# Local-global attention feeding a routed FFN: the first batch without zero-padded queries

## The chip, the cores and the metric

One core of a Trainium2 chip. The metric is the device time of one launch in microseconds, median of the runs shown. A profiled execution also has a span, from the first to the last instruction of the program; times inside it are counted from the span's start.

## The reference, cut to what matters

```python
# q_l, k_l, v_l: [8, 8, 512, 64]; q_g, k_g, v_g: [8, 8, 32, 64]; window 32
s_ll = where(|i - j| <= 32, scale * q_l @ k_l.T, -1e9)      # local rows: a band of keys
s_l  = concat([scale * q_l @ k_g.T, s_ll])                  # and the 32 global keys
out_l = softmax(s_l) @ concat([v_g, v_l])
out_g = softmax(scale * q_g @ concat([k_g, k_l]).T) @ concat([v_g, v_l])
x = concat([out_g, out_l]) per batch, heads side by side    # [4352, 512]
# greedy routing of the 4352 tokens to 8 experts of equal capacity 544, by x @ w_gate,
# then per expert out = relu(x_e @ w1) @ w2
```

## The kernel before, in words

The program has three parts in time: attention (to about 213 us of the span), routing (to about 244 us), and the eight expert FFNs. Each part needs the whole of the one before it.

Attention goes by pairs of heads, (batch b, pair q), q from 0 to 3, so 32 pairs. The host lays out queries and keys of a pair transposed in one array (`qk`: 64 partitions for each head), and the values with the windows of keys side by side (`ve`). For each pair GpSimd spreads the keys into a tile `kx` (three copies, line 117) and makes a shifted copy of the values, `vo` (lines 131 and 132).

The local queries of a head are 16 blocks of 32, and each block meets 128 keys (its own, both neighbours' and the global ones). The scores S of a pair are made in one of two ways:

- `Pair.scores`: for each block and each head one matmul of 64 partitions (the head's 64 dimensions) with 32 query columns: 32 matmuls in tiles of 64x32, which write the two S tiles (one for each head) in turns.
- `Padded.scores`: the queries lie in a tile `qz` of 128 partitions, head 0's in the upper half and head 1's in the lower one, with zeros beside them, so that one matmul of 128 partitions with 64 columns makes a block for both heads: 16 matmuls. GpSimd fills `qz` with two more copies for each such pair (line 121). There are two `qz` tiles, zeroed once at the start.

Which pair is which is said by `pads(b, q)`. A float32 matmul shows in the trace as two MATMUL and two LDWEIGHTS rows, a transpose as one of each.

After the scores VectorE subtracts, masks and takes the row maxima (line 197), ScalarE does the exponentials (line 202), TensorE transposes them (line 92), ScalarE and VectorE copy the transposed halves out of PSUM (line 353, 355), TensorE multiplies with the values (`outs`, from `ve` and `vo`), and VectorE divides by the row sums. Global queries of two pairs go together (`Glob`, tiles `pg`, `pgt`), and `Gate` turns finished rows and multiplies them with the gate weights.

The pairs are staged by hand in the loop over `st`: in stage st TensorE makes the scores of pair st+1, transposes pair st, and multiplies pair st-1 with its values, in that order. Each engine runs its instructions in the order in which they are written.

Loads and stores are issued by SyncE. `pe()` counts TensorE's instructions, 4 for a matmul and 2 for a transpose; when the count passes 194 and then every further 256, the instruction there is noted, and the next loads that `hand()` issues wait until it has run. So the loads go at a pace that the TensorE program sets. Buffers: six each of `qk` and `ve`, four each of `kx` and `vo`, four PSUM tiles S and four OT.

Of the kernel before, what the change touches and what calls it, by code (L numbers as in the profile page):

```python
# [68 lines left out]
def attention(ctx, tc, A, consts, xd, ident, L, nbatch, rt=None):  # L69
# [29 lines left out]
    def load_qk(b, p):  # L99
        t = ld.tile([128, 2 * QW], F32, name="qk", bufs=6)  # L100
        w = kx[(b * NP + p) % NK]
        move(t, A["qk"][b, p])
        k, qk[b, p] = t[:, QW:], (t, w)
        z = padded[b, p] = qz[(b * NP + p) // 2 % NZ] if pads(b, p) else None
        pd = list(w.ap[0])
        own = (ap_of(w[:, 128:192], 0, [pd, [160, 8], [1, 64]]), k[:, :SL].rearrange("p (a b) -> p a b", b=64))
        nxt = (ap_of(w[:, 224:256], 0, [pd, [160, 7], [1, 32]]),
               k[:, 64:SL].rearrange("p (a b) -> p a b", b=64)[:, :, 0:32])
        glo = (ap_of(w[:, 32:64], 0, [pd, [160, 8], [224, 2], [1, 32]]),
               k[:, None, None, SL:].to_broadcast([128, 8, 2, 32]))  # L110

        def spread(*engines):
            for e, (o, i) in zip(engines, (own, nxt, glo)):
                if e is nc.scalar:
                    e.activation(o, i, AF.Copy)
                else:
                    e.tensor_copy(o, i)  # L117
            if z is not None:
                for h in range(2):
                    r = slice(64 * h, 64 * h + 64)  # L120
                    nc.gpsimd.tensor_copy(z[r, :, h, :], t[r, :SL].rearrange("p (j i) -> p j i", i=32))
        return spread
# [10 lines left out]
        return spread  # L133

    def pads(b, q):
        return q % 2 == 0 and b + q > 0

    padded = {}
    qz = [ac.tile([128, NW, 2, 32], F32, name=f"qz{i}") for i in range(NZ)]
# [303 lines left out]

    ns = len(P)
    pairs = [(Padded if pads(*x) else Pair)(*x) for x in P]
    globs, need = {}, list(range(ns))
    for b in range(nbatch):
# [928 lines left out]
```

## Time and profile before

| | |
|---|---|
| runs, us | 689.93, 690.57, 693.05; median 690.57 |
| profiled execution | 688.41 us, span 686.6 us |
| mean granted TensorE clock | 0.974 of full speed |
| TensorE busy | 93% of the span |
| TensorE share of the chain that ended last | 76%; VectorE 13%, DMA 4%, issue 3%, ScalarE 2% |

The profiled execution lies 2.2 us below the median. "Issue" is time in which an engine waited for nothing that the profile shows.

### The profile page before, as it was taken

To read this page: it belongs to the slowest core of one execution; us is meant where nothing else is said; L and a number is where in the kernel's file an instruction comes from. 1 tells how busy PE (TensorE), PEld (TensorE's weight loads), DVE (VectorE), ACT (ScalarE), POOL (GpSimd) and SP (SyncE) were. 2 spreads that over 40 slices of the span, in tenths; PEclk is the share of its full clock that TensorE was granted. 3 is DMA by queue.
4 is the path that set the end of the run, shared out by engine and by line. 5 is a ranking of instruction groups with operands and counts; after the bars stand their busy time and mean duration, and the time that the engine had idled before them with its cause. 6 is when DMAs were issued, how large, how long until landed. Compare 5 with 4: busy or idle time off the path is not lost.

```text
span 686.6 us, 21729 instructions
## 1 busy us (share of the span) xinstructions
PE 635.3 (93%) x8854; PEld 543.9 (79%) x8854; DVE 488.2 (71%) x1988; ACT 315.1 (46%) x863; POOL 248.3 (36%) x321
## 2 busy tenths in 40 slices
PE   7889998899894289999999999999999999999996
PEld 7778876777773179879879978978977988988985
DVE  4697876776787788889988887978977961741510
ACT  5677877767760034344433433443432451642411
POOL 7877687673530050241141142142232143221011
PEclk9999999999998589999999999999999999999999
DMA  8585876776412170243334324325324325522001
GB/s 311 196 286 200 259 242 228 236 234 228 145 59 91 43 262 7 73 155 150 129 98 151 125 85 169 128 81 169 127 81 154 139 71 204 168 89 86 16 20 47
DMA packets 27253, 98.54 MB, mean 144 GB/s; under 512 B 5648, under 2 KB 5904, under 8 KB 23056
## 3 DMA queue, kind: packets, MB, share of 16 engines
q0 software_dynamic: 10640, 52.44, 22.3%
q1 hardware_dynamic: 16512, 44.70, 19.1%
q8 instruction: 70, 1.15, 0.7%
q14 instruction: 31, 0.25, 0.1%
HBM read 79.30 MB, written 17.83 MB: 141 GB/s over the span
## 4 chain that ended last, share of the span: by engine, by line
PE 76%; DVE 13%; DMA 4%; issue 3%; ACT 2%; POOL 0%; SPq 0%; POOLq 0%; DVEq 0%; ACTq 0%
PE H L1228 26%; PE Y L1254 25%; PE S L89 7%; PE OT L92 6%; PE OT L89 6%; PE R L716 3%; PE H L1054 2%; DVE p L197 2%; PE Y L1244 2%; DMA xg<-xd,idx 1%; DVE xs L232 1%; DMA qk<-in_qk_dram 1%; DMA w1r<-in_w_dram,widx 1%; DMA w2r<-in_w_dram,widx 1%; DVE pt L355 1%
## 5 line engine op out<-in xcount | busy, mean ns | idle before, releaser
L1228 PE MATMUL H<-xh,w1h 128*128 128x272 f32 (+2 forms) x512 | 149.2, 292 | 0.9 <-ACT xh L1027 0.8
L1228 PE MATMUL H<-xh,w1l 128*128 128x272 f32 (+2 forms) x512 | 149.7, 293 | 0.3 <-DVE w1l L641 0.3
L1228 PE MATMUL H<-xl,w1h 128*128 128x272 f32 (+2 forms) x512 | 148.6, 291 | 0.2 <-DVE xl L641 0.2
L1254 PE MATMUL Y<-w2h,hh 128*128 128x512 f32 x256 | 104.1, 407 | 0.0
L1254 PE MATMUL Y<-w2h,hl 128*128 128x512 f32 x256 | 103.3, 403 | 0.0
L1254 PE MATMUL Y<-w2l,hh 128*128 128x512 f32 x256 | 103.2, 403 | 0.0
L1231 ACT ACTIVATE hh<-H 128x272 fp32r<-128x272 f32 (+2 forms) x128 | 50.9, 398 | 113.2 <-PE H L1228 108.5
L1228 PEld LDWEIGHTS H<-xh,w1h 128*128 128x128 f32 x512 | 96.7, 189 | 1.7 <-ACT xh L1027 1.1
L1228 PEld LDWEIGHTS H<-xl,w1h 128*128 128x128 f32 x512 | 96.4, 189 | 0.8 <-DVE xl L641 0.6
L1228 PEld LDWEIGHTS H<-xh,w1l 128*128 128x128 f32 x512 | 96.6, 189 | 0.4 <-DVE w1l L641 0.4
L202 ACT ACTIVATE p<-p,nm 128x128 f32<-128x128 f32 x256 | 78.1, 398 | 2.5 <-DVE nm L197 2.5
L1014 POOL DMA_INDIRECT xg<-xd,idx x40 | 39.6, 989 | 103.2 <-DVE idx L641 47.9
L197 DVE CUSTOM_DVE_ANT_0 p<-S,mask 128x128 f32<-128x128 f32 x256 | 58.1, 286 | 20.2 <-PE S L89 17.7
L641 DVE SCALAR_TENSOR_TENSOR hl<-H,hh 128x272 fp32r<-128x272 f32 (+2 forms) x128 | 54.9, 434 | 20.5 <-ACT h L1233 14.0
L641 DVE TENSOR_TENSOR w2l<-w2r,w2h 128x512 fp32r<-128x512 f32 x64 | 41.8, 684 | 30.6 <-ACT w2h L1027 30.2
L1190 ACT ACTIVATE y<-Y 128x512 f32<-128x512 f32 x32 | 19.2, 599 | 94.8 <-PE Y L1254 80.9
L117 POOL COPY kx<-qk 128x512 f32<-128x512 f32 (+1 forms) x93 | 46.0, 530 | 43.8 <-DMA qk<-in_qk_dram 26.3
L1066 POOL DMA_INDIRECT out_dram<-y,idx x32 | 32.3, 1010 | 76.7 <-ACT y L1190 40.0
L1254 PEld LDWEIGHTS Y<-w2h,hh 128*128 128x128 f32 x256 | 48.3, 189 | 10.3 <-issue 1.6
L1254 PEld LDWEIGHTS Y<-w2h,hl 128*128 128x128 f32 x256 | 48.3, 189 | 9.2
L1254 PEld LDWEIGHTS Y<-w2l,hh 128*128 128x128 f32 x256 | 48.4, 189 | 8.9
L1027 ACT ACTIVATE w1h<-w1r 128x512 fp32r<-128x512 f32 x64 | 37.1, 624 | 35.3 <-DMA w1r<-in_w_dram,widx 35.3
(183 smaller groups left out, 1311.0 us busy)
## 6 DMA issues: line engine op xcount, KB each, us to landing
qk<-in_qk_dram SPq DMA_DIRECT2D x32, 544.0 KB
ve<-in_vw_dram SPq DMA_DIRECT2D x32, 520.0 KB
xd<-xs SPq DMA_DIRECT2D x32, 256.0 KB
xg<-xd,idx POOLq DMA_INDIRECT x40, 3.4
mask<-in_mask_dram SPq DMA_DIRECT2D x1, 512.0 KB
cf<-in_cf_dram POOLq DMA_DIRECT2D x1, 512.0 KB, 7.4
xd<-xg SPq DMA_DIRECT2D x16, 32.0 KB
gx<-xd POOLq DMA_DIRECT2D x8, 64.0 KB, 3.6
```

Source lines behind the costliest of these rows:

```text
L89: return pe(nc.tensor.matmul(*args, **kw), 4)
L92: return pe(nc.tensor.transpose(*args), 2)
L117: e.tensor_copy(o, i)
L197: nc.vector.tensor_tensor_reduce(s.p[h][:, c, :], s.st[h][:, c, :], mask[:, s.band(h, c), :], -SCALE, BIG, ALU.add, ALU.min, s.nm[h][:, c: ...
L202: nc.scalar.activation(s.p[h][:, c, :], s.p[h][:, c, :], AF.Exp, bias=s.nm[h][:, c:c + 1], scale=-1.0)
L641: return op(*args, **kw)
L1014: nc.gpsimd.indirect_dma_start(out=dst, out_offset=None, in_=src, element_offset=off, in_offset=bass.IndirectOffsetOnAxis(ap=idx, axis=0))
L1027: nc.scalar.activation(hi, raw, AF.Copy)
L1066: nc.gpsimd.indirect_dma_start(out=out, out_offset=bass.IndirectOffsetOnAxis(ap=rt.rows(ph, t)[:n], axis=0), in_=y[:n], in_offset=None)
L1228: nc.tensor.matmul(p, w[d][:, fs], x[:, d, q], start=(k == 0), stop=(k == 11))
L1231: nc.scalar.activation(hh[:, f, q], p, AF.Relu)
L1254: nc.tensor.matmul(p, h[:, f, q], w[f], start=(f + k == 0), stop=(f + k == 9))
```

## The change

`pads(b, q)` was true for every even pair but the very first, (0, 0). It is now true for even pairs from the second batch on. So it alters one pair, (0, 2), the third of the program, which becomes a `Pair` where it was a `Padded`. With it go its two copies into `qz`, its mask slices are those of the first third of `mask`, and its two halves are heads where they were halves of the sequence. `qz` tiles and their zeroing stay.

```diff
     def pads(b, q):
-        return q % 2 == 0 and b + q > 0
+        return q % 2 == 0 and b > 0
```

On TensorE, at the third group of scores, the tiles named are keys (`kx`), queries (`qk`, or padded `qz`), exponentials (`p`, `pg`):

```order
 L89 MATMUL S<-kx_103,qk 32x32 x2
 L92 MATMUL OT<-ident,p 128x128 x8
-L89 MATMUL S<-kx_104,qz_97 64x128 x16
+L89 MATMUL S<-kx_104,qk 32x128 x32
 L92 MATMUL OT<-ident,p 128x128 x4
 L92 MATMUL OT<-ident,pg_106 128x128 x6
```

Sixteen matmuls become 32, at the same place; in the trace 32 MATMUL rows become 64, and everything behind them stands 32 such rows, or 64 instructions, later in TensorE's stream.

On GpSimd, at the copies for pair (0, 2) and the shifted values of pair (0, 0):

```order
 L117 COPY kx_104<-qk 128x7x32
 L117 COPY kx_104<-qk 128x8x2x32
-L121 COPY qz_97<-qk 64x16x32 x2
 L131 COPY vo_98<-ve 128x1040
 L132 COPY vo_98<-ve 32x2x455
```

Two copies go, nothing else moves on this engine in attention.

On SyncE, the first place at which the order of loads differs (after the first store of global rows, `xd<-xg`):

```order
 L95 DMA ve<-in_vw_dram 128x1040 x2
 L349 DMA xd<-xg 4x32x64
+L95 DMA qk<-in_qk_dram 128x1088
+L95 DMA ve<-in_vw_dram 128x1040
 L95 DMA qk<-in_qk_dram 128x1088 x2
-L95 DMA ve<-in_vw_dram 128x1040 x2
 L349 DMA xd<-xg 4x32x64
```

Since `pe()` counts 64 more from pair (0, 2) on, the marks fall on instructions that stand earlier, and `hand()` takes the loads in another order from there on.

## Rows read from the trace of the kernel before

**Rows 1.** The page: TensorE's busy time and instructions.

```profile
PE 635.3 (93%) x8854; PEld 543.9 (79%) x8854; DVE 488.2 (71%) x1988; ACT 315.1 (46%) x863; POOL 248.3 (36%) x321
```

**Rows 2.** Busy time by stretch (us:us length, engines, PEclk, DMA share, GB/s).

```profile
33.00:213.40 180.40, 164.70 (x4675) 135.48 (x4653) 139.66 (x779) 129.34 (x404) 109.64 (x164) 1.00 0.63 208
213.40:244.20 30.80, 10.36 (x219) 7.70 (x219) 23.89 (x95) 2.12 (x4) 3.10 (x4) 0.56 0.16 53
```

**Rows 3.** TensorE in order of time (start, length, engine, line, [idle before]).

```profile
5.49 1.16 PE L89 MATMUL S<-kx,qk 64*32 64x128 f32 x64
12.25 3.54 PE L89 MATMUL S<-kx,qz 128*64 128x128 f32 x32 [1.99 <-POOL qz L121]
18.45 2.08 PE L89 MATMUL S<-kx,qk 64*32 64x128 f32 x80
22.85 0.41 PE L89 MATMUL OT<-ve,pgt 128*32 128x64 f32 x16
25.58 0.22 PE L89 MATMUL OT<-vo,pt 128*32 128x65 f32 x1 [1.91 <-issue]
26.04 3.47 PE L89 MATMUL S<-kx,qz 128*64 128x128 f32 x32
37.89 1.97 PE L89 MATMUL S<-kx,qz 128*64 128x128 f32 x32
...
112.34 0.22 PE L89 MATMUL OT<-vo,pt 128*32 128x65 f32 x1 [2.00 <-issue]
```

**Rows 4.** GpSimd in order of time, the first 22 us.

```profile
9.49 1.49 POOL L117 COPY kx<-qk 128x512 f32<-128x512 f32 x3 [2.41 <-DMA qk<-in_qk_dram]
10.92 1.28 POOL L121 COPY qz<-qk 64x512 f32<-64x512 f32 x2
...
14.50 1.48 POOL L117 COPY kx<-qk 128x512 f32<-128x512 f32 x3 [0.19 <-DMA qk<-in_qk_dram]
...
17.93 0.71 POOL L654 DMA_DIRECT2D cf<-in_cf_dram  x1
...
20.11 1.28 POOL L121 COPY qz<-qk 64x512 f32<-64x512 f32 x2
```

**Rows 5.** Granted clock (the number after POOL) and DMA share by stretch.

```profile
12.25:15.50 3.25, 3.25 (x30) 3.25 (x32) 0.93 (x8) 1.72 (x6) 2.99 (x5) 0.50 0.93 384
...
25.80:29.10 3.30, 3.30 (x43) 3.13 (x35) 1.69 (x11) 0.04 (x1) 3.18 (x6) 0.50 0.63 200
```

**Rows 6.** The whole program's instruction queue (packets, MB, share).

```profile
q8 instruction: 70, 1.15, 0.7%
```

**Rows 7.** Busy time from one code stall to the fourth after it.

```profile
93.64:112.33 18.69, 16.11 (x504) 13.87 (x505) 14.11 (x81) 14.29 (x46) 11.97 (x19) 1.00 0.76 256
```

**Rows 8.** TensorE's waits for "issue" in 33 to 215 us (total, times, longest).

```profile
PE S L89 <- issue: 5.2, 8, 1.1
PE OT L89 <- issue: 4.1, 4, 2.0
```

**Rows 9.** VectorE in order of time: the last maximum of pair (0, 1).

```profile
11.01 0.08 DVE L197 DVE_READ_ACCUMULATOR2_ANT nm<- 128x1 f32 x1
```

**Rows 10.** Instruction packets in 10.5 to 11.6 us, then in 22.9 to 24.1 us.

```profile
q8 instruction: 1, 0.02, 5.3%
...
q8 instruction: 1, 0.02, 5.1%
```

**Rows 11.** DMA share, second number from the end, in two stretches.

```profile
12.00:15.30 3.30, 3.05 (x30) 3.05 (x32) 0.93 (x8) 1.97 (x7) 2.99 (x5) 0.52 0.98 403
15.30:17.80 2.50, 2.50 (x48) 2.14 (x50) 1.22 (x9) 1.38 (x4) 2.44 (x4) 0.96 0.09 28
```

**Rows 12.** SyncE's load queue: the first load behind the second mark.

```profile
17.78 0.33 SPq L95 DMA_DIRECT2D qk<-in_qk_dram  x1
```

**Rows 13.** Granted clock around two other long idle times.

```profile
48.00:52.00 4.00, 2.55 (x122) 2.12 (x121) 3.85 (x23) 2.40 (x10) 3.88 (x7) 1.00 0.91 352
...
113.40:117.00 3.60, 3.60 (x68) 3.26 (x68) 2.63 (x18) 1.66 (x4) 3.48 (x6) 1.00 0.36 92
```

## The prediction, made before the changed kernel had run

> **What bounds the kernel now.** I read the views from the whole to the part. The page has TensorE busy for 93% of the span [rows 1]. The busy times by stretch then show two regimes: through attention from 33 us on TensorE works 164.7 of 180.4 us, more than VectorE, ScalarE or GpSimd, and the DMA engines are busy 63%; in routing TensorE works a third of the time and waits for VectorE [rows 2]. Routing and the FFNs start from attention's last result, so whatever TensorE gains in attention and keeps to its end comes off the whole. The change alters only the first 26 us of it directly, so I read TensorE in order of time there [rows 3]. Three things stand out: it waits 1.99 us for `qz` before the changed pair's scores; these 32 rows take 3.54 us, against 1.97 us for the same 32 rows later on; and 13 us later it stops for 1.91 us with nothing to wait for ("issue"), after which the next padded scores are slow again (3.47 us). [...]
>
> **What the issue stalls are.** The instruction queue of the DMA moved 70 packets in 1.15 MB, so 16 KB each [rows 6]. TensorE ran 8854 matmul rows and as many weight loads [rows 1]: 17,708 / 70 = 253 instructions to a packet. Between the stalls that end at 93.64 and at 112.34 lie 504 matmul rows and 505 weight loads [rows 7], four packets of 252, so 126 matmul rows to a block; the rest to the packet are waits that the trace doesn't count. Blocks end at a fixed place in TensorE's stream, and a stall is code that came late. Two stalls tell how late: the packet that the stall at 25.58 needed moved within 22.9 to 24.1 us [rows 10], so its code was usable about 1.5 us later [rows 3]. Over the rest of attention such stalls make 5.2 + 4.1 = 9.3 us [rows 8].
>
> **The change, step by step, on TensorE's time.**
>
> *The wait for `qz`.* GpSimd has `kx` of the pair ready at 9.49 + 1.49 = 10.98 us and then fills `qz` for 1.28 us [rows 4]; that copy goes. The plain form writes both S tiles in turns, so it also needs the last maximum of pair (0, 1) read, 11.09 us [rows 9]. Scores start at about 11.15 instead of 12.25: **-1.10 us**.
>
> *The scores.* 64 plain rows took 1.16 us at the higher clock level [rows 3]; instead of 3.54: **-2.38**. At the lower level twice 1.16 would save 1.2, and against padded scores at the higher level 1.97 - 1.16 = 0.81; these are the bounds.
>
> *Code, first block.* Counting rows along the timeline, 472 have run at the stall of 25.58; 126 and 252 rows back block ends lie at rows 346 and 220. Row 220 stood behind the transposes; now it is the 48th of the 64 new rows, reached at 11.15 + 48 x 0.018 = 12.0. Its packet moved within 10.5 to 11.6 [rows 10], usable 1.5 later, about 12.95: **+0.95** (0 if its code is usable at once, 1.9 if it is as late as at 25.58).
>
> *The next keys.* `kx` of pair (0, 3) is ready at 14.50 + 1.48 = 15.98 in both, since that copy waits for its load [rows 4]: the 1.28 us that GpSimd saves turn into waiting for `qk`. TensorE, now 2.53 us ahead of 18.45, would be there at 15.92: **+0.1**. So this load is the cover that would eat any larger gain here.
>
> *Code, second block.* Row 346, the end of the scores of (0, 3) before, is now in their middle, reached at 16.0 + 0.57 = 16.6. [...]
>
> *Code, third block.* The packet for the stall at 25.58 was late because it met loads: the two behind the second mark, the first of them issued at 17.78 [rows 12], and the routing constants issued at 17.93 [rows 4]. Now `pe()` passes that mark at the 27th of the new matmuls (344 + 108 = 452 of 450) instead of the fourth of the following `outs`, so these loads (1.06 MB, 2.7 us at the 403 GB/s of [rows 11]) go out at about 13 and are done by 18. [...]
>
> *The clock of pair (1, 0).* Its scores ran at the lower level behind that stall, 3.47 us instead of 1.97, and begin at about 22.9 now (`qz` is ready at 21.39 [rows 4]): **-1.5** (0 if the clock falls nevertheless).
>
> The sum is -1.10 - 2.38 + 0.95 + 0.1 + 1.2 - 1.91 - 1.5 = **-4.6 us** against this execution. Yet its clock isn't that of every run: of three idle times near 2 us, two were followed by the lower level, the third, 2.00 us at 112.34, by 1.00, as was an idle 4.00 - 2.55 = 1.45 us in 48 to 52 us [rows 3, 5, 13]. So I count the lower level at two in three: the scores then save 2/3 of 2.38 plus 1/3 of 0.81 = 1.85, and the last term is -1.0, which gives **-3.6 us**. [...]
>
> From 26 us on the same work runs earlier by that. The 64 instructions shift every later block end and mark by a quarter of a block against the work. This moves the 9.3 us of stalls about; the same stretches recur in each batch with block ends at ever other places, so I take the total as unchanged, with 2 to 3 us either way.
>
> [...]
>
> **Rivals.**
> 1. *The gain is given back at once.* If the third packet is late in any case and the clock falls again behind it, the last two terms go: -4.6 + 1.9 + 1.5 = -1.2 us. For it: the DMA engines are 63% busy all through attention [rows 2], so another load may take the place of the moved ones. [...]
> 2. *Slower.* The shifted blocks end at worse places in batches 1 to 7. A block of plain scores alone would run in 126 x 0.018 = 2.3 us, and waits for whatever its code needs beyond that. From 9.3 us the stalls would have to reach 9.3 + 3.6 + 3.5 = 16.4 us for the kernel to be slower by over 0.5%; from 12.9 us on it is no faster. For it: marks and loads move too, in another order. Against: blocks come at all places already.
> [...]
> 4. *More.* The 32-row shift happens to clear some of the 9.3 us: three of the long stalls gone is -7 us.
>
> **How the numbers follow.** The execution of 688.41 us has 1.8 us outside its span of 686.6; nothing there changes. It lies 2.2 us under the median, and the -3.6 us are for runs in general, so I forecast 690.57 - 3.6 = **686.9 us**. Chances: the forecast's mechanism with a net of -2 to -5.5 us, 0.45; rival 1, 0.2 (689.4); rival 2 down to no gain 0.1, beyond +0.5% 0.07; rival 3, 0.04; rival 4, 0.14 (683.5). 0.5%, 3.45 us, is about what this measurement tells from no change, so the forecast lies on the line between faster and same: faster gets rival 4 and somewhat over two thirds of the forecast's share, 0.46; same 0.47; slower 0.07. The range 682.5 to 691.0 leaves out the far ends of rivals 2 and 4.
>
> **What would show it.** Right: scores of (0, 2) from about 11.2 us in 64 rows, broken by an issue stall near 12 us; a second one near 16.6 in those of (0, 3); none near 22 to 25; PEclk at 1.0 to 33 us; pair (1, 0) scored from about 23 us; TensorE waiting for `kx` or loads nowhere. The routing begins 3 to 5 us earlier than 213.4. Wrong: the clock at 0.50 in these 33 us again; a stall of 1.5 us or more at the third block; issue stalls behind 33 us far from 9.3 us.

## The result, and the profile after

The changed kernel takes 698.94 us (median of 5 runs, 696.77 to 699.80), against 690.57 us before on the same chip: a ratio of 1.0112, with a 95% interval of 1.0079 to 1.0145. The forecast was 686.9 us, and 698.94 lies outside its range. The change makes the kernel slower by 8.4 us; between the two profiles 7.8 of 9.1 us lie in attention.

The profiled execution took 697.52 us. From its page, TensorE's busy time and instructions (answers to [rows 1]): the 32 matmul rows are there, and 2.6 us more of busy time, although the new rows are shorter than the old.

```profile
PE 637.9 (92%) x8886; PEld 546.3 (79%) x8886; DVE 488.4 (70%) x1988; ACT 315.2 (45%) x863; POOL 247.0 (35%) x319
```

Busy time by stretch, first to where attention ends now (its last step is at 221.6 us, where it was at 213.8), then the stretch of [rows 2]. TensorE's granted clock, third number from the end, is 0.97 where it was 1.00 (in the traces of both kernels it has two levels, 1.00 and 0.50), and in the same 180.4 us TensorE gets through 4539 rows, not 4675.

```profile
33.00:221.20 188.20, 168.44 (x4697) 140.10 (x4686) 140.00 (x780) 130.15 (x406) 109.88 (x165) 0.97 0.60 200
33.00:213.40 180.40, 162.71 (x4539) 135.97 (x4532) 135.28 (x764) 128.81 (x404) 109.38 (x164) 0.97 0.61 202
```

**The first 30 us.** TensorE in order of time, answers to [rows 3]:

```profile
11.65 1.00 PE L89 MATMUL S<-kx,qk 64*32 64x128 f32 x47 [1.39 <-POOL kx L117]
12.81 0.48 PE L89 MATMUL S<-kx,qk 64*32 64x128 f32 x17 [0.16 <-issue]
...
16.32 0.67 PE L89 MATMUL S<-kx,qk 64*32 64x128 f32 x32 [0.31 <-POOL kx L117]
21.09 2.92 PE L89 MATMUL S<-kx,qk 64*32 64x128 f32 x48 [4.09 <-issue]
...
28.05 1.97 PE L89 MATMUL S<-kx,qz 128*64 128x128 f32 x32
```

The scores of (0, 2) begin at 11.65 and end at 13.29 us, where they ended at 12.25 + 3.54 = 15.79. Those of (0, 3) begin at 16.32 instead of 18.45: TensorE is 2.1 us ahead. Then, after 32 of their rows, it stops for 4.09 us with nothing to wait for. The 48 rows behind it run at half clock (0.50), and the scores end at 24.01 instead of 20.53, 3.5 us behind. The old stall of 1.91 us before the `outs` is gone and the scores of (1, 0) run in 1.97 instead of 3.47 us, so they end at 30.02, where they ended at 29.51: all that was gained is lost, and 0.5 us more.

What held the code back stands in the load queue and in the DMA share. SyncE issues the two loads behind the second mark 4.5 us earlier than in [rows 12]:

```profile
13.28 0.33 SPq L95 DMA_DIRECT2D qk<-in_qk_dram  x1
13.65 0.43 SPq L95 DMA_DIRECT2D ve<-in_vw_dram  x1
```

The stretches behind (the last three numbers are clock, DMA share, GB/s; [rows 11] had 0.09 from 15.3 to 17.8):

```profile
13.30:18.00 4.70, 3.39 (x110) 2.79 (x110) 3.72 (x23) 4.46 (x15) 3.44 (x6) 1.00 1.00 380
18.00:19.00 1.00, 0.00 (x0) 0.00 (x0) 0.00 (x0) 0.00 (x0) 0.96 (x3) 1.00 0.48 179
...
19.10:25.80 6.70, 4.71 (x57) 3.38 (x58) 2.73 (x19) 0.71 (x2) 6.46 (x11) 0.50 0.56 173
```

The DMA engines are full to 18.0 us. The instruction packet that TensorE needs is moved at 18.70, 5.9 us after the block before had ended near 12.8, and the code is used from 21.09. TensorE, idle since 17.00, gets the lower clock level, 0.50, from 19.0 to 25.9 us.

**The rest of attention.** TensorE's waits for "issue" from 45 us to its end (total, times, longest), answers to [rows 8]:

```profile
PE S L89 <- issue: 8.7, 6, 2.5
...
PE OT L89 <- issue: 4.1, 2, 2.1
...
PE OT L92 <- issue: 1.3, 2, 0.9
```

They make 14.1 us in 10 stalls, where 12 made 9.2 (9.3 as a sum of the rounded rows). The four longest:

```profile
47.94 0.81 PE L89 MATMUL S<-kx,qk 64*32 64x128 f32 x40 [2.43 <-issue]
...
66.43 0.30 PE L89 MATMUL OT<-vo,pt 128*32 128x65 f32 x2 [2.06 <-issue]
...
130.76 0.98 PE L89 MATMUL S<-kx,qz 128*64 128x128 f32 x14 [2.49 <-issue]
...
157.88 0.22 PE L89 MATMUL OT<-ve,pt 128*32 128x65 f32 x1 [2.00 <-issue]
```

Behind the last three of them the granted clock is at its lower level, 0.50, for 3.4 us each (66.8 to 70.2, 131.7 to 135.1, 159.0 to 162.4). In the first profile of the kernel before it never was in this part of attention; in a second one, further down, it was once (110.5 to 113.9).

The third of them in detail. TensorE enters the block ahead of the code that is late at 130.76 at 125.42, and the packet is moved at 128.40, 3.0 us behind that. (Counted in rows, the packets of both traces up to attention's end move 0.2 to 5.9 us behind such an entry, with two exceptions: at 15.95 us in the kernel before, 1.5 us ahead of it, and at 74.18 us now, as TensorE enters.) In the kernel before, this block begins and ends 32 rows further in the same work, at 122.66 and 127.52, and its end has no stall. The stretch of this one block, first in the changed kernel, then before:

```profile
125.42:128.27 2.85, 2.85 (x128) 2.52 (x128) 2.58 (x16) 2.85 (x13) 2.67 (x5) 1.00 0.96 362
```

```profile
122.66:127.52 4.86, 4.86 (x128) 4.59 (x129) 4.16 (x27) 4.16 (x15) 4.58 (x7) 1.00 0.93 330
```

Both hold as many rows, at the same clock, with the DMA engines over 90% busy. But the shift gives the block 32 quick rows of `outs` at its front and takes 32 slow ones from its end, padded scores and transposes: it keeps TensorE busy for 2.85 us instead of 4.86. Before, the packet came at 124.61, 1.95 us after the block's start. With 2.01 us more of work to cover it, 0.5 of the 2.49 us of the stall would be left, by this estimate. So at this place the shifted ends left 2.85 us of work instead of 4.86 ahead of the next code, and with the DMA engines 96% busy that code was first used 5.34 us after the block's start (125.42 to 130.76).

**The sum.** From profile to profile attention's end moves by +7.8 us. Its first gate product, which is a fixed place in the work, comes at 43.92 instead of 42.84, +1.1; from there to the end are 177.6 instead of 170.9, +6.7, of which 4.8 are issue stalls. Beside them TensorE's busy time in this part grows by 2.9 us, with the three stretches at the lower clock in it, and its other waits shrink by 1.0. Routing takes 0.8 and the FFNs 0.5 us more. That is 9.1, the difference of the spans (695.7 and 686.6).

### The profile page after: what moved, and what is told of

It reads as the page before. It is cut to its first block, busy times and chain, and to the rows that moved or that the text cites. A ratio compares the mean times of both kernels' runs of the same rounds, so it can differ in the third digit from the quotient of the medians.

```text
span 695.7 us, 21791 instructions
## 1 busy us (share of the span) xinstructions
PE 637.9 (92%) x8886; PEld 546.3 (79%) x8886; DVE 488.4 (70%) x1988; ACT 315.2 (45%) x863; POOL 247.0 (35%) x319
## 4 chain that ended last, share of the span: by engine, by line
PE 80%; DVE 8%; DMA 5%; issue 4%; ACT 1%; POOL 1%; POOLq 0%; ACTq 0%; DVEq 0%
PE H L1228 26%; PE Y L1254 24%; PE S L89 9%; PE OT L92 7%; PE OT L89 7%; PE R L716 3%; PE Y L1244 2%; PE H L1054 2%; DMA xg<-xd,idx 2%; DMA qk<-in_qk_dram 1%; DVE p L197 1%; DMA w1r<-in_w_dram,widx 1%; DMA w2r<-in_w_dram,widx 1%; DVE r_G L641 1%; DVE r_pm L641 1%
## 5 line engine op out<-in xcount | busy, mean ns | idle before, releaser
L197 DVE CUSTOM_DVE_ANT_0 p<-S,mask 128x128 f32<-128x128 f32 x256 | 58.0, 286 | 24.1 <-PE S L89 23.5
```

Of the source, the lines that this page charges most:

```text
L197: nc.vector.tensor_tensor_reduce(s.p[h][:, c, :], s.st[h][:, c, :], mask[:, s.band(h, c), :], -SCALE, BIG, ALU.add, ALU.min, s.nm[h][:, c: ...
```

## The experiments

**Theory A:** the 64 instructions shift the code blocks' ends, and the load marks, against the work, and what it costs is code that comes late, in the first batch and in those behind. **Theory B:** something in the plain scores or in the new state of the first batch itself costs the time. "Late stalls" are TensorE's waits for issue from the first gate product to attention's end, in the profiled execution. In the table "moved" is against the work as it is in the kernel before. The kernel before was run again beside each group of experiments, with medians of 689.08 to 691.00 us; the ratios in the text are to these.

| kernel | pair (0, 2) | block ends | marks | first gate product | attention's end | late stalls, us (times) | median us |
|---|---|---|---|---|---|---|---|
| before | padded | as before | as before | 42.84 | 213.8 | 9.2 (12) | 690.57 |
| before, again | padded | as before | as before | 39.64 | 214.1 | 10.5 (14) | 691.33, one run |
| changed | plain | moved | moved | 43.92 | 221.6 | 14.1 (10) | 698.94 |
| e1 | plain | moved | as before | 42.80 | 222.7 | 16.0 (13) | 696.70 |
| e3 | padded | moved | as before | 40.87 | 219.3 | 17.4 (15) | 695.87 |
| e2 | padded | moved | moved | 42.89 | 219.6 | 13.8 (10) | 691.45 |
| e2, again | padded | moved | moved | 40.38 | 216.2 | 15.2 (11) | 693.02, one run |
| e4 | padded | as before | moved | 38.05 | 214.9 | 16.4 (13) | 692.22 |
| e5 | plain | as before | as before | 43.44 | 216.2 | 9.6 (12) | 693.66 |
| e7 | plain | back at (1, 1) | back at (1, 1) | 43.97 | 217.7 | 10.8 (15) | 692.65 |
| e6 | plain | back at (1, 1) | as before | 44.34 | 216.8 | 9.9 (12) | 694.17 |
| e9 | plain | back at (1, 1) | back at (1, 1) | 41.10 | 214.3 | 10.6 (12) | 690.98 |
| e8 | plain | back at (1, 1) | as before | 39.74 | 213.6 | 9.4 (13) | 687.84 |

**The marks put back (e1).** The changed kernel, but each matmul of (0, 2) counts 2, so that every mark stands at the same work as before; the block ends stay moved.

```diff
-    mm(s.st[h]..., start=True, stop=True)
+    pe(nc.tensor.matmul(s.st[h]..., start=True, stop=True), 2 if (s.b, s.q) == (0, 2) else 4)
```

> Pair (0, 2) plain as in the changed kernel, but its 32 matmuls count 2 instead of 4 for the loads' marks, so that every mark stands at the same place in the work as in the kernel before; the ends of the code blocks stay shifted by 64 instructions. Theory A1 (the two loads that the earlier mark sends out at 13 us hold up the code packet): the stall of 4.1 us near 21 us shrinks to about 1.2 us, the clock stays at 1.00 there, and the time is 690 to 694 us. Theory A2 (the shifted block ends alone cost the time, all through attention): the late issue stalls stay near 14 us and the time near 696 us. Theory B (the plain scores themselves, small tiles that keep TensorE less busy, cost the time): 698 us.

696.70 us, ratio 1.0080 (1.0044 to 1.0116). The early part of theory A holds: TensorE in order of time has

```profile
18.17 0.67 PE L187 MATMUL S<-kx,qk 64*32 64x128 f32 x32 [1.03 <-issue]
22.57 0.38 PE L89 MATMUL OT<-ve,pgt 128*32 128x64 f32 x11 [0.21 <-issue]
23.39 1.97 PE L89 MATMUL S<-kx,qz 128*64 128x128 f32 x32
```

So the moved loads made the stall of 4.09 us: with them back the packet is moved at 15.95 us instead of 18.70 and the stall is 1.03, and the scores of (1, 0) end at 25.36, 4.15 us ahead of before. But by the first gate product this lead is gone (a stall of 2.18 us at 37.01, and half clock behind it), and the late stalls are 16.0 us.

**Block ends moved alone (e3), marks moved alone (e4), both (e2)**, in the kernel before with its padded scores. e3 puts 16 tiny matmuls (64 instructions) ahead of the scores of (0, 2), in a tile that the scores then overwrite, and doesn't count them; e2 counts them; e4 puts none in but counts the padded matmuls of (0, 2) double.

```diff
+                if (s.b, s.q, u) == (0, 2, 0):
+                    for _ in range(16):
+                        nc.tensor.matmul(s.st[u][0:32, 0, 0:16], warm[:, 0:32], warm[:, 0:16], start=True, stop=True)
```

> The kernel before with 16 tiny matmuls on zeros ahead of the padded scores of pair (0, 2), not counted for the marks: only the ends of the code blocks are shifted by 64 instructions from there on. Theory A (the late issue stalls follow from where block ends and marks lie in the work): they come at the places where the changed kernel and the two shifted ones before had them and sum to 13 to 17 us behind 43 us, not 9 as in the kernel before; the time is 692 to 698 us. Theory C (the late stalls differ from run to run whatever the places, and the profile of the kernel before was a lucky one): 9 to 16 us at no particular places.

> The kernel before, with the 16 padded matmuls of pair (0, 2) counted as 8 instead of 4, so that the marks stand as in the changed kernel while block ends and work are those of before. Theory A with the marks as the cause: 694 to 699 us. Theory A with the block ends as the cause, or theory B: 688 to 692 us.

> The kernel before, with pair (0, 2) padded, and 16 tiny matmuls on zeros ahead of its scores (64 instructions, counted for the marks), which TensorE can do while it waits for qz. So block ends and marks stand as in the changed kernel from there on, and the work is that of before. Theory A: late issue stalls near 14 us and 695 to 700 us. Theory B: 690 us.

> The padded work with 16 tiny matmuls put in that shift both block ends and marks (as in the earlier run of the same kernel, whose profiled execution was its slowest by 5 us and had 13.8 us of late issue stalls). If that execution was typical in its stalls, they are 13 to 15 us again and the span is near 695; if the kernel's usual 691 us come from fewer stalls, they are 9 to 11 and the span is near 690.

e3 is the clearest: 695.87 us, ratio 1.0116 (1.0083 to 1.0150), the whole loss without a single plain score of (0, 2). Its waits for issue from 45 us on:

```profile
PE S L89 <- issue: 8.8, 6, 3.3
PE OT L89 <- issue: 7.7, 7, 1.8
...
PE OT L92 <- issue: 1.0, 2, 0.7
```

e4 has 692.22 us, ratio 1.0048 (1.0004 to 1.0092): no issue stall up to its first gate product, which comes 4.8 us earlier than in the first profile of before, and 16.4 us of late stalls, which take that back and more. e2 has as many late stalls as the changed kernel in both its profiles, but 691.45 us, ratio 1.0010 (0.9977 to 1.0042), in runs that spread from 687.81 to 696.51. So late stalls alone don't make the 8.4 us, and the time of e2 is near what theory B expected (690), not A (695 to 700).

Which block ends have a stall does follow from where they lie. Counted in rows of TensorE's stream, all 13 late stalls of e1, with plain scores, fall at block ends at which e3, with padded ones, has one of its 15. The two profiles of e2 have 9 and 10 of the 10 of the changed kernel; the kernel before has stalls at 4 of these places in its stream.

**Plain scores, blocks and marks as before from (0, 2) on (e5).** Five of the ten warm-up matmuls are replaced by 53 tiny ones: 48 matmuls more are 192 instructions, which with the 64 of (0, 2) make 256, about one whole block: in the trace of the kernel before TensorE has 17,708 rows and 180 waits and drains for the 70 packets, so 255.5 to a packet. So ahead of (0, 2) the block ends are moved, and behind it they fall at the same work as before; the counts are set so that no mark moves.

```diff
-    for _ in range(WARM):
-        mm(wt[:, 0, :], warm, warm, start=True, stop=True)
+    for _ in range(5):
+        pe(nc.tensor.matmul(wt[:, 0, :], warm, warm, start=True, stop=True), 8)
+    for _ in range(53):
+        nc.tensor.matmul(wt[0:32, 1, 0:16], warm[:, 0:32], warm[:, 0:16], start=True, stop=True)
```

> Pair (0, 2) plain, marks as in the kernel before, and 192 more instructions in the warm-up (5 large and 53 tiny matmuls instead of 10 large ones, on zeros, not counted for the marks), so that with the 64 of the plain scores the block ends lie at the same places in the work as before from pair (0, 2) on. Theory A (places of block ends and marks): issue stalls behind 33 us near 9.3 us as before, and 685 to 690 us, since only the direct gain of 2 to 4 us is left. Theory B (the plain scores themselves): 697 to 699 us.

693.66 us, ratio 1.0032 (1.0001 to 1.0062), above the 685 to 690 that theory A expected. The new warm-up holds the start back by 3.8 to 4.9 us, and by 30 us the kernel is 0.6 us behind, so some 4 us were regained there. Late stalls are 9.6 us in 12: with the places of the kernel before, plain scores bring no more of them.

**The loads taken away (quiet before, quiet after).** Both kernels, with loads of the 7th pair onward cut to a sliver.

> The kernel before with every load of queries, keys and values from the seventh pair on cut to a twelfth or less (64 columns of 1088, 65 of 1040; the rest of the six buffers keeps what earlier pairs left), so that the DMA engines are nearly idle from some 28 us on; the output is not the reference's. Theory A in the form that code comes late because its packets meet loads: the late issue stalls fall from 9.2 us to under 4 us and the time to 678 to 685 us. If code is late by its own latency, they stay at 7 us or more.

> The changed kernel with the same loads cut; the output is not the reference's. Theory A: the second mark's loads are still full here, so the early stall near 21 us stays, but the late stalls fall as in the quiet kernel before, and the two differ by less than 3 us where they differ by 8 with all loads. Theory B (the plain scores themselves): this one stays 6 to 9 us slower than the quiet kernel before.

682.94 us, ratio 0.9929 (0.9900 to 0.9959), and 685.23 us, 0.9950 (0.9921 to 0.9979). Waits of TensorE from 45 us on, of the first and of the second:

```profile
PE S L88 <- issue: 2.3, 3, 1.0
PE OT L88 <- issue: 0.8, 1, 0.8
```

```profile
PE S L88 <- issue: 3.5, 5, 1.1
PE OT L88 <- DMA ve<-in_vw_dram: 2.1, 1, 2.1
```

Their DMA share in attention behind 33 us is 0.21, not 0.63, and the late stalls fall to 3.1 and 3.5 us: about two thirds of the stalls before, and three quarters of those after, are gone with the loads that their packets would meet. The loads of the first six pairs are whole, and with them the early stall (3.15 us at 20.16); the two medians differ by 2.3 us where they differed by 8.4. The profiles are of executions of 680.12 and 687.24 us. With late stalls nearly alike, the second takes 5.1 us longer from the first gate product to attention's end: 2.1 of it are the wait for `ve`, and TensorE's busy time is 1.2 more, with 3.4 us at the lower clock in it. So stalls for code aren't all that moves these times.

**The kernel before once more.**

> The kernel before, unchanged, profiled a second time. Theory A: late issue stalls of 8 to 11 us at the same places as in its first profile. Theory C: the sum may as well be 13 to 16 us.

Late stalls 10.5 and, in its first 40 us, no half clock: the first gate product comes 3.2 us earlier than in the first profile. So single profiles of one kernel differ by this much up to there, and by 1.3 us in late stalls; all 12 stalls of the first are there again. Against this profile the changed kernel is 4.3 us later at the first gate product and loses 3.2 us behind it, so the split of the 7.8 us given above is that of one pair of profiles.

**Pair (1, 1) padded as well (e7, e6).** It takes 64 instructions out again, so that from there on blocks end where they did before; e6 sets the counts so that no mark moves.

```diff
-        return q % 2 == 0 and b > 0
+        return q % 2 == 0 and b > 0 or (b, q) == (1, 1)
```

> The changed kernel with pair (1, 1) made from padded queries too, so that 64 of TensorE's instructions go again there: from (1, 1) on the code blocks end, and the marks fall, at the same work as in the kernel before; between (0, 2) and (1, 1) they stand as in the changed kernel. Theory A (the places of block ends and marks decide): the stall of about 4 us near 21 us stays, attention's first gate product comes 0 to 1.5 us later than before, the issue stalls behind it fall from 14.1 us to 9 to 10.5, at the rows of work where they lay before, and the time is 690 to 693 us. Theory B (the plain scores themselves cost the time, or something else in the first batch): nothing gets better by padding a later pair, 697 to 700 us.

> As the run before with (1, 1) padded too, and the counts of (0, 2) and (1, 1) written so that every mark stands at the same work as in the kernel before; then the load marks never move, and the block ends stand elsewhere only from (0, 2) to (1, 1). Theory A: the early stall is about 1 us as with the marks put back alone, so attention is 3 to 4 us ahead at 30 us, the late issue stalls are 9 to 10.5 us as before, and the time is 686 to 689 us, less than either kernel. Theory B: no better than with the marks put back alone, 696 to 698 us. If the late stalls are at 14 us in spite of equal block ends and marks, what decides is not the places but how far ahead the work runs of its loads, and A falls in that form.

In both kernels (1, 0) and (1, 1) share a `qz` tile, so the queries of (1, 1) replace those of (1, 0) before its scores are made: these scores are computed from the queries of (1, 1), and they wait for the copies. In e6:

```profile
26.77 0.69 PE L249 MATMUL S<-kx,qz 128*64 128x128 f32 x4 [3.46 <-POOL qz L121]
```

That wait eats the early gain: 692.65 us, ratio 1.0039 (1.0013 to 1.0065), and 694.17, 1.0047 (1.0021 to 1.0073). The late stalls are 10.8 and 9.9 us as theory A expects, but the time of e6 isn't what it expects (686 to 689); a `qz` tile for (1, 1) alone tells whether that wait is the reason.

**With a `qz` tile of its own for (1, 1) (e9, e8).** A third tile, zeroed by GpSimd after the keys of (0, 1).

```diff
-        z = padded[b, p] = qz[(b * NP + p) // 2 % NZ] if pads(b, p) else None
+        z = padded[b, p] = qz[2 if (b, p) == (1, 1) else (b * NP + p) // 2 % 2] if pads(b, p) else None
```

> The same without the counts: marks between (0, 2) and (1, 1) as in the changed kernel, so the loads go out at 13 us and the early stall of 3 to 4 us near 20 us comes back. Theory A: first gate product within 1 us of before, late issue stalls 9 to 11 us, 690 to 693 us. Theory B: 694 to 699.

> Pair (1, 1) padded too, with a third qz tile of its own, and the counts of (0, 2) and (1, 1) written so that every mark stands at the same work as before. From (1, 1) on block ends and marks are those of the kernel before. Theory A (their places decide): no wait for qz at (1, 0); attention 3 to 4 us ahead of before at 30 us; issue stalls behind the first gate product 9 to 10.5 us at the rows of before; 686 to 689 us, so 2 to 4 below the kernel before. Theory B (the plain scores, or running ahead of the loads, cost the time): late issue stalls or waits for loads grow by what was gained early, and the time is 690 to 693.

e9: 690.98 us, ratio 1.0010 (0.9982 to 1.0038). Against the changed kernel it makes one later pair padded (with GpSimd's zeroing and copies for it), and the ratio to the kernel before is 1.0010, not 1.0112. In the two profiles 2.8 us of this come before the first gate product (the early stall was 2.61 us here, and the clock stayed up), and 4.5 us behind it, where the block ends are back. e8: 687.84 us, ratio 0.9975 (0.9948 to 1.0003). In order of time and in the waits from 45 us on it shows:

```profile
13.51 0.48 PE L187 MATMUL S<-kx,qk 64*32 64x128 f32 x17 [0.97 <-issue]
17.79 0.67 PE L187 MATMUL S<-kx,qk 64*32 64x128 f32 x32 [0.47 <-issue]
22.74 0.38 PE L89 MATMUL OT<-ve,pgt 128*32 128x64 f32 x11 [0.76 <-issue]
23.83 1.70 PE L249 MATMUL S<-kx,qz 128*64 128x128 f32 x28
```

```profile
PE OT L89 <- issue: 5.9, 6, 2.4
...
PE S L187 <- issue: 1.6, 2, 0.8
...
PE S L249 <- issue: 1.5, 3, 0.8
```

Three small early stalls, the scores of (1, 0) at 23.8 instead of 26.0, and the late stalls of the kernel before. On the median this is 2.4 us below the kernel before, of the 3.6 that were forecast, but the interval just reaches 1, so that there is no gain isn't ruled out. Of all kernels run with their full loads it has the lowest median.

**What follows.** For the late stalls theory A holds and B falls. The table divides without overlap: where ends and marks stand as before behind (1, 1), six kernels and seven profiles have 9.2 to 10.8 us of late stalls; where either is moved, five kernels and six profiles have 13.8 to 17.4. The time from the first gate product to attention's end divides in the same way: 170.9 to 174.4 us against 175.8 to 179.9. For the whole time, e3 has the loss without the plain scores, and e8 and e9 keep them without it, so the plain scores by themselves aren't its cause. But e2, with ends and marks both moved, has no loss on the median: that the moved places account for all of the 8.4 us isn't shown.

## Why the prediction was wrong

*Right, nearly to the term:* the wait for `qz` and the scores. They were to begin at 11.15 and end at 13.26 with a stall of 0.95 between; they began at 11.65, since `kx` came later, the stall was 0.16, and they ended at 13.29. The next keys: (0, 3) was to begin at 16.02 and did at 16.32. Third block and clock of (1, 0), -1.91 and -1.5: the stall is gone, and 3.47 became 1.97.

*Wrong, the first: the +1.2 for the code of the second block.* No run shows this term; the changed kernel showed a stall of 4.09 us in its place, and half clock behind it, for 48 of the 80 rows, made these take 3.59 instead of 2.08 us, another 1.5. The DMA share of 0.09 behind 15.3 us [rows 11] is that of the trace of before, while the step on the third block moves 1.06 MB of loads into that stretch. They take it to 1.00 up to 18.0, and the packet goes behind them. In the kernel before this very packet is moved at 15.95 us, 1.5 us ahead of the entry into the block before it (row 220, at 17.42). With the marks back (e1) the stall is 1.03 and the lead at 30 us 4.15, so the sum of -4.6 was near that of a kernel whose loads stay. Nor does a run show the times by which the -1.91 of the third block and the start of (1, 0) at 22.9 were set: that packet was moved at 22.23, the stall is gone, and these scores began at 28.05. The loads were indeed out of the third packet's way, by being in the second's.

*Wrong, the second: the 9.3 us of stalls "unchanged, with 2 to 3 us either way".* They are 14.1. "The same stretches recur with block ends at ever other places" took the arrangement of before for a middling one. By late stalls it is the best of the four that the table holds (ends moved, marks moved, both, neither), and the others have 13.8 to 17.4 us. Rival 2 named this mechanism and its direction, with chances of 0.1 and 0.07. Its point of 16.4 us for slower by 0.5% assumed an early gain of 3.6; without that the point is 12.8, and the late stalls were over it.

In sum, on the profiles: -4.6 forecast, +9.1 measured, 13.7 apart: 5.7 to the first gate product, 4.8 of late stalls, 1.9 more in attention beside them, 1.3 behind it. Part of the first of these is the spread between executions: the second profile of the kernel before reaches its first gate product 3.2 us earlier than the one that the forecast started from.

*Rival 1* (the gain given back at once) happened too, by the second packet and not by the third. Late code cost 4.09 us at one place, and 3.1 to 17.4 us in the batches behind in every kernel run here; most block ends have no stall, though: in the changed kernel 10 of some 35 have a late one.

*Open:* why e2, moved in both ways, is on the median at 691.45, 7.5 us below the changed kernel, with late stalls as large. Its first gate product comes 1.0 and 3.5 us earlier in two profiles, and it spends 10.2 and 6.8 us at half clock in attention, where the changed kernel spends 17.1; that points to the clock, but the spread of 8.7 us between its runs was not explained. Which block ends matter most was not tried one by one either.

## What to carry to other kernels

TensorE's code came in blocks of 126 matmul rows here, and 64 instructions more in its stream (32 rows) moved every later block end against the work; in such a case put in as many do-nothing instructions (e3) or take as many out right behind (e8) to see the edit apart from the shift. In a kernel that has been through many such choices, the arrangement in place is probably better than a random one, so a shift counts as a loss, not as nothing: here 5 to 8 us more of late code in single profiles, and 0.1 to 1.2% of the time. And when one step of a prediction moves loads, read the DMA share anew for every other step, since the trace of before no longer shows it.

## What the runs showed of the hardware

- Code packets came late where the DMA engines were full of loads: with them full from 13.3 to 18.0 us (share 1.00) a packet was moved 5.9 us after the block end (12.8 to 18.70), with them at 30% (127.50 to 130.09 in the kernel before) after 0.8 us (127.52 to 128.35). Without most loads (DMA share 0.21, not 0.63) late stalls fell from 9.2 to 3.1 us.
- In the changed kernel TensorE's granted clock went to 0.50 behind idle times of 4.09, 2.06, 2.49 and 2.00 us, for 6.9 us the first time and 3.4 the others, but stayed at 1.00 behind the 2.43 us that end at 47.94. At the first, 48 rows of plain scores took 2.92 us, where 80 took 2.08 at the higher level.
- Rows in 64x32 tiles: in the changed kernel 47 took 1.00 us from 11.65, 21 ns each, at a granted clock of 1.00.
